# Attention loop of a recurrent-attention and mixture-of-experts kernel: the decay scans, the copies of T's blocks and one group of constants change their places and size

## The chip, the cores and the metric

One core of a Trainium2 chip. The metric is the device time of one execution in microseconds; lower is better. Engines: PE (TensorE), DVE (VectorE), ACT (ScalarE), POOL (GpSimd) and SP (SyncE, which issues most transfers).

## The reference

Three programs follow one another: a recurrent attention over 768 steps for 32 heads with a state of 40x40 each, a mixture of 8 experts with one expert for each token, and a dense network with squared ReLU.

```python
for t in range(S):
    y[:, :, t] = np.einsum('bhd,bhde->bhe', rt, state)
    Sa = np.einsum('bhde,bhe->bhd', state, at)
    state_decay = state * wt[:, :, None, :] - np.einsum('bhd,bhe->bhde', Sa, bt)
    state = state_decay + np.einsum('bhd,bhe->bhde', vt, kt)
...
x = np.ascontiguousarray(attn_out.transpose(0, 2, 1, 3)).reshape(B * S, H * D)
x = _moe_ref(x=x, **moe_kwargs)
return _moe2_ref(x=x, **moe2_kwargs)
```

## The kernel before

**Tiling.** The attention works in 24 chunks of 32 steps; all 32 heads of a chunk are treated together. Inside a chunk the recurrence becomes matrices of 32x32 per head. Of each chunk the kernel needs: the products of the decays from both ends of the chunk (`scan`, two scans on DVE of 104x512, L157 and L163, with L160 and L162 between them), the inputs scaled by them (`scale`, L175 to L177, three products on POOL; for m >= 2 L175 is DVE's), a gram matrix on PE with a mask (`gram` L191, `gram_mask` L206 on ACT and L207 on DVE), and the inverse T of a triangular matrix. T is worked out for four chunks at once, spread over four iterations (`inv_start`, `inv`: products L261 on DVE and POOL, sums L265 on DVE, and at the end a transpose on DVE, L300, into the tile TT). `block_T` (L309) copies the blocks of one chunk from TT into the block-diagonal tile TB with four copies on ACT; `solve` (L386, px) multiplies with it.

**Order.** The order of the instructions on every engine is the order in which the code is written (`manual_schedule`): no scheduler moves anything. Each engine takes its own instructions in that order and waits for others by semaphores. The loop in `run` goes over c from 0 to 22, m is c % 4, and LA is 7. Iteration c works on several chunks at once: the state, the scores and the output y of chunk c; T's use (`solve`) for chunk c+1; the natural-order copies (`nat_n`, `nat_a`) and `block_T` of chunk c+2; the gram of chunk c+7; the scan and the scaling of chunk c+8 (nothing from c=16 on, since there are 24 chunks).

**One iteration, in PE's order.** u1 (L401) and state_t (L453), nat_k (L337, pk), u (L417), solve (L386, px), state (L437, ps), vu_t (L467, pv), gram (L191), scores (L479, pq), the transposes of x for the gate (L805, gpt), a group of constants (L519, `warm`), the gate's logits (L819, pl), a second group of constants, y (L497), the transposes pa (L337), and a third group at the head of the next iteration; a fourth one stands ahead of u. `warm` multiplies a tile of constants and writes a tile of PSUM that nothing reads.

**ACT's order around the change.** The logits' copy (L820), two copies into X (L332, L333), the copies of pa (L349, L350, L358), T's blocks (L309, four copies into TB), then the next iteration's copies into ru (L406), rhsY (L457), vu (L422), rhsY (L375), lu (L389), vut (L470).

**DVE's order around the change.** The state's update (L441), the gram's mask (L207), the two scans, the mask of the scores (L483, which y needs as its operand rq), and then, by m: in m=0 the inverse's first products, with the scans behind the mask of the scores; in m=1 four sums of the inverse; in m=2 L175, the last sums and products and the transpose L300; in m=3 the gate's choice (L840 to L848), L175 and the ranks. At the end of an iteration stands x (L506). In m=3, and in some late iterations, PE counts the experts (L857, pc) between pa and the next u1, and ACT copies the counts (L859, pr).

**Queues.** SP loads the operands of later chunks (E, wB, R, V) in code order; a load waits until the readers of its buffer are done. POOL scatters the rows of x (L901).

Of the kernel before, what the change touches and what calls it, by code (L numbers as in the profile page):

```python
# [35 lines left out]
class Attention:  # L36
# [484 lines left out]
    def run(self, extra, weights):  # L521
        LA = 7
# [4 lines left out]
        def wload(i):  # L527
            r = (self.L, self.Tt)[i % 2].rearrange("p a b -> p (a b)")
            weights.load(i, r[:, 0:704], 1)
# [57 lines left out]
        idle = gate.mats.rearrange("p a b -> p (a b)")  # L587
        late, LM = None, 0

        def warm0(i):  # L590
            if c == 0:
                self.warm(W2[i], self.zt, 320, True)

        for c in range(NC - 1):
            m = c % 4
            warm0(0)
            bt = gate.batch(c)
            if c:
                self.warm(1, idle, 256, True)
            self.u1(c)  # L600
            if c:
                self.state_t(c)
            self.nat_k(c + 1)
            if c:
                self.warm(1, idle, 256, True)
            self.u(c)
            self.nat_kc(c + 1)
            self.solve(c + 1)
            if bt and 17 <= c:
                gate.choose(*bt)  # L610
            warm0(1)
            if c == 0:
                self.gram(5)
                self.gram_mask(5)
                self.scale(6, (V, G, V))
            if m:
                self.load_r(c + 1)
                self.load(c + LA + 2)
            if c in FILL:
                extra(*FILL[c])  # L620
            if c >= 21:
                gate.xT(c - 1)
            if c == 22:
                self.warm(1, idle, 256)
            self.state(c)
            if m == 0:
                self.load_r(c + 1)
                self.load(c + LA + 2)
            if c == 0:
                self.scan(7)  # L630
                self.scale(7, (V, G, G))
            self.vu_t(c)
            if c:
                self.gram(c + LA)
                self.gram_mask(c + LA)
                if m == 0:
                    self.inv_start(c // 4 + 1, lambda k, h: G)
                self.inv(PLAN[m][0])
            else:
                PLAN0 = PLAN[0][0] + PLAN[0][1]  # L640
                warm0(2)
                self.gram(6)
                self.gram_mask(6)
                warm0(3)
            if m:
                self.scan(c + LA + 1)
            self.scores(c)
            if c < 21:
                gate.xT(c - 1)
            if c:  # L650
                self.warm(1, idle, 256)
            gate.logits(c - 1)
            if c == 0:
                warm0(4)
                self.gram(7)
                self.gram_mask(7)
                warm0(5)
                self.inv_start(1, lambda k, h: G)
            if bt and c < 17:
                gate.choose(*bt)  # L660
            self.load_v(c + 2)
            if c:
                self.store_x(c - 1)
            if m == 0:
                self.scan(c + LA + 1)
            self.scale(c + LA + 1, (G, V, G) if m >= 2 else None)
            self.load_w(c + LA + 4)
            if bt:
                if c == 22:
                    self.warm(1, idle, 256)  # L670
                if c >= 17:
                    gate.count(*bt)
            if c:
                self.warm(1, idle, 512)
            self.y(c)
            self.nat_n(c + 2)
            self.nat_a(c + 2)
            self.nat_pc(c + 2)
            if bt and c < 17:
                gate.count(*bt)  # L680
            self.inv(PLAN[m][1] if c else PLAN0)
            self.block_T(c + 2)
            if late and m == LM:
                gate.rank_batch(*late)
            late = bt if bt and c < 17 else late if m != LM else None
            if c >= 21:
                self.gate_in(c, x22 if c == 22 else None)
            if bt:
                gate.rank(*bt)
                if 17 <= c < 22:  # L690
                    gate.rank_batch(*bt)
            if c < 21:
                self.gate_in(c)
            gate.scatter(1 if c < 20 else 2)
            for i in range(2):
                if 20 <= c < 22:
                    weights.prep(2 * c - 40 + i, i == 0)
                if 19 <= c < 21:
                    wload(2 * c - 38 + i)
            if c == 21:  # L700

                one, iota = (self.p2.tile([128, 512], F32, tag="wB", name=f"io{i}", bufs=3)[:, 0:NS1] for i in range(2))
                V.memset(one, 1.0)
                V.tensor_tensor_scan(iota, one, one, -1.0, ALU.mult, ALU.add)
                T1 = self.eb(6, [128, DM + 2 * NS1], F32)
                x22, oh22, oh23 = T1[:, 0:DM], T1[:, DM : DM + NS1], T1[:, DM + NS1 :]
        c = NC - 1
# [921 lines left out]
```

## Time and profile before

| what | value |
|---|---|
| median of 3 runs | 1175.13 us (1173.62 to 1182.4) |
| the profiled execution | 1179.27 us, of which the span from first to last instruction is 1177.6 us |
| busy over the span | PE 1022.5 us (87%), DVE 685.8 (58%), ACT 613.4 (52%), POOL 286.1 (24%) |
| mean granted TensorE clock | 0.925 of full speed |

All times in the rows below are from that one execution. An instruction group of a timeline row has its start, its length, engine, line, operation, output and inputs, count, and in brackets how long the engine was idle ahead of it and what ended that. PE's busy time counts pipelined matmuls whose ends are modelled. The granted clock is a share of 2.4 GHz; its only other level is 1.2 GHz (0.50), so a value between is a mix over the stretch.

### The profile page before, as it was taken

Reading aid. Unit: us, or ns where it says so; the run is one execution under the profiler, and the core shown is the slowest. Engines: PE = TensorE matmul, PEld = TensorE weight load, DVE = VectorE, ACT = ScalarE, POOL = GpSimd, SP = SyncE. Lnnn points to the kernel's source line nnn. Section 1 sums busy time; section 2 is a strip of 40 time slices with the busy share of each in tenths; the row PEclk is TensorE's granted clock in tenths of the full one; section 3 lists DMA queues with packets and bytes.
Section 4 is the critical chain, followed back from the end, with each engine's and each line's share of the span. In section 5 each row is a group of like instructions: output and inputs, shape, how many; then the busy total and the mean of one; then the engine's idle time right before and its main releaser. Section 6 shows DMA issues by size and latency. Waiting matters only on the chain.

```text
span 1177.6 us, 33048 instructions
## 1 busy us (share of the span) xinstructions
PE 1022.5 (87%) x13806; PEld 889.1 (76%) x13806; DVE 685.8 (58%) x1435; ACT 613.4 (52%) x1402; POOL 286.1 (24%) x338
## 2 busy tenths in 40 slices
PE   5376897787897888879988999989999999999996
PEld 3255676575676766667888999878899999999995
DVE  7964645675475364345688787886744444344432
ACT  7156457475565666852555555545644444444431
POOL 5423113123123120001265554541430101000000
PEclk7588869999789799997999999989999999999998
DMA  7737326344343122212676676652310101000000
GB/s 208 196 91 237 83 75 181 87 134 137 98 120 91 45 77 88 88 40 71 184 229 211 210 218 210 196 161 82 89 56 12 34 12 35 13 11 13 11 13 25
DMA packets 75087, 122.86 MB, mean 104 GB/s; under 512 B 8790, under 2 KB 56520, under 8 KB 72432
## 3 DMA queue, kind: packets, MB, share of 16 engines
q1 hardware_dynamic: 72624, 112.87, 33.1%
q0 software_dynamic: 2304, 7.78, 2.0%
q8 instruction: 110, 1.80, 0.6%
q14 instruction: 49, 0.40, 0.1%
HBM read 91.36 MB, written 29.35 MB: 103 GB/s over the span
## 4 chain that ended last, share of the span: by engine, by line
PE 56%; ACT 15%; DVE 12%; issue 5%; DMA 3%; POOL 1%; SPq 0%; ACTq 0%; DVEq 0%; POOLq 0%
PE phg L1292 15%; PE pog L1318 5%; PE pog L1317 5%; PE pog L1316 5%; PE phe L1292 4%; PE px L386 3%; ACT ru L406 3%; PE warm L519 2%; ACT TB L309 2%; ACT rhsY L457 2%; DVE e L163 2%; PE ps L437 2%; DVE rq L483 2%; ACT vut L470 1%; PE pa L337 1%
## 5 line engine op out<-in xcount | busy, mean ns | idle before, releaser
L1302 DVE SCALAR_TENSOR_TENSOR sqg<-phg,rg 128x512 f32<-128x512 f32 x96 | 66.3, 691 | 119.1 <-ACT rg L1301 115.6
L441 DVE TENSOR_TENSOR ru<-ps,Pc 40x640 f32<-40x640 f32 x46 | 37.8, 822 | 142.1 <-PE ps L437 141.7
L1301 ACT ACTIVATE rg<-phg 128x512 f32<-128x512 f32 x96 | 57.3, 596 | 110.7 <-PE phg L1292 110.5
L1304 DVE TENSOR_TENSOR hlg<-sqg,hhg 128x512 fp32r<-128x512 f32 x96 | 66.6, 694 | 65.9 <-ACT hhg L1303 61.1
L1303 ACT CAST hhg<-sqg 128x512 fp32r<-128x512 f32 x96 | 59.6, 620 | 78.6 <-DVE sqg L1302 75.4
L1292 PE MATMUL phg<-xhg,e 128*128 128x512 f32 x264 | 93.1, 393 | 0.0
L519 PE MATMUL warm<-mats 128*128 128x256 f32 x204 | 82.4, 496 | 1.4 <-ACT pr L859 1.4
L386 PE MATMUL px<-TB,X 128*112 128x128 f32 x384 | 59.9, 321 | 24.5 <-DVE N L207 15.3
L386 PEld LDWEIGHTS px<-TB,X 128*112 128x112 f32 x384 | 54.8, 216 | 27.4 <-DVE N L207 15.5
L1318 PE MATMUL pog<-e,hlg 128*128 128x320 f32 x240 | 74.2, 309 | 0.0
L1317 PE MATMUL pog<-e,hhg 128*128 128x320 f32 x240 | 74.1, 309 | 0.0
L1316 PE MATMUL pog<-e,hhg 128*128 128x320 f32 x240 | 74.0, 308 | 0.0
L176 POOL TENSOR_TENSOR e<-e,wB 104x512 f32<-104x512 f32 x21 | 35.7, 1700 | 121.3 <-PE warm L519 84.5
L1110 POOL TENSOR_TENSOR e<-rw,e 128x256 fp32r<-128x256 f32 x51 | 43.3, 853 | 70.0 <-ACT e L1109 56.0
L1292 PE MATMUL phe<-xhe,e 128*128 128x480 f32 (+4 forms) x176 | 59.2, 377 | 0.0
L1292 PEld LDWEIGHTS phg<-xhg,e 128*128 128x128 f32 x264 | 49.6, 188 | 8.9
L1318 PE MATMUL poe<-e,hle 128*120 128x320 f32 (+4 forms) x150 | 47.3, 316 | 5.9 <-DVE hle L1297 5.9
L1292 PE MATMUL phg<-xlg,e 128*128 128x512 f32 x132 | 51.8, 392 | 0.0
L1296 ACT ACTIVATE hhe<-phe 128x480 fp32r<-128x480 f32 (+4 forms) x64 | 33.8, 529 | 34.1 <-PE phe L1292 33.8
L1431 POOL DMA_INDIRECT x2g<-zs_s,idx x24 | 23.7, 988 | 113.6 <-ACT hhg L1303 105.7
L191 PE MATMUL G<-e 64*32 64x64 f32 (+1 forms) x1536 | 23.7, 245 | 29.3 <-issue 15.1
L417 PEld LDWEIGHTS pu<-ru,lu 128*32 128x32 f32 x1536 | 19.6, 125 | 38.7 <-ACT ru L406 32.3
(330 smaller groups left out, 2995.8 us busy)
## 6 DMA issues: line engine op xcount, KB each, us to landing
e<-in_E_dram SPq DMA_DIRECT2D x24, 832.0 KB
rw<-in_w_dram SPq DMA_DIRECT2D x30, 320.0 KB
rw<-in_w_dram SPq DMA_DIRECT2D x30, 256.0 KB
zs_s<-zt SPq DMA_DIRECT2D x4, 1600.0 KB
ru<-in_VR_dram SPq DMA_DIRECT2D x48, 128.0 KB
cr<-in_wi_dram SPq DMA_DIRECT2D x20, 256.0 KB
cr<-in_wo_dram SPq DMA_DIRECT2D x20, 256.0 KB
wB<-in_E_dram SPq DMA_DIRECT2D x23, 208.0 KB
```

The lines of the kernel that those rows point to most:

```text
L386: self.nc.tensor.matmul(px[0:112, par, 128 * o : 128 * o + 128], X[:, par, o, :], TB[:, 4 * par + o, :], start=True, stop=True)
L441: V.tensor_tensor(rUn[s, par, :, :, 0:40].rearrange("p (h q) z d -> p h (q z) d", h=2), ps[s, :, 0:320].rearrange("p h (a d) -> p h a d", ...
L519: self.nc.tensor.matmul(w[:, i % 2, 0:cols], r[:, 0:128], r[:, 0:cols], start=True, stop=True)
L1110: (V if own else self.nc.gpsimd).tensor_tensor(W["l1"], r1, b32(W["h1"]), ALU.subtract)
L1292: T.matmul(o, lt, rt, start=(i == 0), stop=(i == len(seq) - 1))
L1301: A.activation(r[:, :n], o, AF.Relu)
L1302: V.scalar_tensor_tensor(sq[:, :n], o, 0.0, r[:, :n], ALU.max, ALU.mult)
L1303: A.copy(hh[:, :n], sq[:, :n])
L1304: V.tensor_tensor(hl[:, :n], sq[:, :n], b32(hh)[:, :n], ALU.subtract)
L1316: T.matmul(o, hh[:, t], W["h2"], start=(f == 0), stop=False)
L1317: T.matmul(o, hh[:, t], W["l2"], start=False, stop=False)
L1318: T.matmul(o, hl[:, t], W["h2"], start=False, stop=(f == NF - 1))
```

## The change

Three edits in the loop of `run`. `scan(c + LA + 1)` stands, for every m, behind the scores, the logits, the gate's choice and the loads; before, only m=0 had it there, and m=1 to 3 had it ahead of the scores. `block_T(c + 2)` stands directly behind the logits for m=0, 1 and 3; for m=2 it stays behind the inverse, which ends there. The second group of constants, between the logits and y, has 256 columns instead of 512.

```diff
-            if m:
-                self.scan(c + LA + 1)
             self.scores(c)
             if c < 21:
                 gate.xT(c - 1)
             if c:
                 self.warm(1, idle, 256)
             gate.logits(c - 1)
+            if m != 2:
+                self.block_T(c + 2)
...
             if c:
                 self.store_x(c - 1)
-            if m == 0:
-                self.scan(c + LA + 1)
+            self.scan(c + LA + 1)
             self.scale(c + LA + 1, (G, V, G) if m >= 2 else None)
...
             if c:
-                self.warm(1, idle, 512)
+                self.warm(1, idle, 256)
             self.y(c)
...
             self.inv(PLAN[m][1] if c else PLAN0)
-            self.block_T(c + 2)
+            if m == 2:
+                self.block_T(c + 2)
```

DVE's rows in iteration c=5 (m=1), from the state's update to x, before (the scans are printed as SCALAR_TENSOR_TENSOR; rq is the masked scores, Xm an inner tile of the inverse):

```order
L441 TENSOR_TENSOR ru_119<-ps_2489,Pc_597 40x16x40 x2
L207 TENSOR_TENSOR N_2576<-G_2543,mL 128x384
L157 SCALAR_TENSOR_TENSOR wB_1591<-wB_1591,onesB 104x512
L160 TENSOR_TENSOR Pc_2586<-wB_1591,e_2167 104x16
L162 RECIPROCAL zR<-Pc_2586 104x16
L163 SCALAR_TENSOR_TENSOR e_2167<-e_2167,zR 104x512
L483 TENSOR_TENSOR rq_126<-pq_2590,mQ 64x512 x2
L265 TENSOR_REDUCE Xm<-pr_7_2579 128x32
```

and of the changed kernel:

```order
L441 TENSOR_TENSOR ru_119<-ps_2489,Pc_597 40x16x40 x2
L207 TENSOR_TENSOR N_2576<-G_2543,mL 128x384
L483 TENSOR_TENSOR rq_126<-pq_2585,mQ 64x512 x2
L157 SCALAR_TENSOR_TENSOR wB_1591<-wB_1591,onesB 104x512
L160 TENSOR_TENSOR Pc_2628<-wB_1591,e_2167 104x16
L162 RECIPROCAL zR<-Pc_2628 104x16
L163 SCALAR_TENSOR_TENSOR e_2167<-e_2167,zR 104x512
L265 TENSOR_REDUCE Xm<-pr_7_2579 128x32
```

The mask of the scores L483 stands directly behind the gram's mask L207, and the four rows of the scan follow it.

DVE's rows in iteration c=6 (m=2), up to the transpose into TT, before:

```order
L441 TENSOR_TENSOR ru_120<-ps_2818,Pc_783 40x16x40 x2
L207 TENSOR_TENSOR N_2905<-G_2872,mL 128x384
L157 SCALAR_TENSOR_TENSOR wB_1928<-wB_1928,onesB 104x512
L160 TENSOR_TENSOR Pc_2915<-wB_1928,e_2486 104x16
L162 RECIPROCAL zR<-Pc_2915 104x16
L163 SCALAR_TENSOR_TENSOR e_2486<-e_2486,zR 104x512
L483 TENSOR_TENSOR rq_125<-pq_2919,mQ 64x512 x2
L175 TENSOR_TENSOR e_2486<-e_2486,wB_1928 104x16x32
L265 TENSOR_REDUCE Tt<-pr_11_2908 128x8x4
L265 TENSOR_REDUCE Tt<-pr_12_2910 128x8x4
...
L300 STREAM_TRANSPOSE TT<-Tt 128x32x32
```

and of the changed kernel:

```order
L441 TENSOR_TENSOR ru_120<-ps_2818,Pc_783 40x16x40 x2
L207 TENSOR_TENSOR N_2905<-G_2872,mL 128x384
L483 TENSOR_TENSOR rq_125<-pq_2914,mQ 64x512 x2
L157 SCALAR_TENSOR_TENSOR wB_1932<-wB_1932,onesB 104x512
L160 TENSOR_TENSOR Pc_2953<-wB_1932,e_2486 104x16
L162 RECIPROCAL zR<-Pc_2953 104x16
L163 SCALAR_TENSOR_TENSOR e_2486<-e_2486,zR 104x512
L175 TENSOR_TENSOR e_2486<-e_2486,wB_1932 104x16x32
L265 TENSOR_REDUCE Tt<-pr_11_2908 128x8x4
L265 TENSOR_REDUCE Tt<-pr_12_2910 128x8x4
...
L300 STREAM_TRANSPOSE TT<-Tt 128x32x32
```

The same rows stand ahead of the transpose L300; L175 now follows the scan L163 directly, where the mask L483 stood between them.

ACT's rows from the last copy of pa in iteration c=4 to the copies into X in c=5, before:

```order
L358 COPY Pn_2327<-pa_2316 128x320
L309 COPY TB_117<-TT 32x8x32 x4
L406 COPY ru_120<-pu_2367 16x8x40 x4
...
L820 COPY lg<-pl_2618 128x8
L332 COPY X_114<-N_901 128x4x48
L333 COPY X_114<-N_901 128x4x48
```

and of the changed kernel:

```order
L358 COPY Pn_2331<-pa_2320 128x320
L406 COPY ru_120<-pu_2367 16x8x40 x4
...
L820 COPY lg<-pl_2613 128x8
L309 COPY TB_118<-TT 32x8x32 x4
L332 COPY X_114<-N_905 128x4x48
L333 COPY X_114<-N_905 128x4x48
```

Between the copy of pa L358 and L406 no block copies are left; those of the next chunk stand behind the logits' copy L820 and ahead of the copies into X.

## Rows read from the trace of the kernel before

**Rows 1.** The page: chain that ended last, whole span, by engine
```profile
PE 56%; ACT 15%; DVE 12%; issue 5%; DMA 3%; POOL 1%; SPq 0%; ACTq 0%; DVEq 0%; POOLq 0%
```

**Rows 2.** Waits, 150 to 520 us: engine, line, waited for: us, times, longest
```profile
ACT X L349 <- PE pa L337: 54.5, 18, 4.8
```

**Rows 3.** Stretches by iteration: us; PE, PEld, DVE, ACT, POOL busy; clock; DMA; GB/s
```profile
138.54:162.71 24.17, 21.78 (x445) 17.67 (x446) 10.78 (x29) 12.24 (x32) 3.71 (x3) 0.72 0.34 91
226.74:245.16 18.42, 15.84 (x443) 12.77 (x443) 11.31 (x31) 11.61 (x30) 3.54 (x3) 1.00 0.42 117
245.16:264.26 19.10, 15.75 (x435) 12.90 (x437) 17.41 (x37) 12.21 (x30) 7.44 (x7) 0.91 0.42 117
264.26:284.38 20.12, 14.89 (x435) 11.83 (x437) 8.88 (x17) 12.20 (x30) 7.78 (x7) 1.00 0.58 178
387.62:411.68 24.06, 21.78 (x445) 18.02 (x447) 11.29 (x30) 13.45 (x33) 4.51 (x4) 0.72 0.17 54
463.14:479.80 16.66, 13.84 (x371) 11.03 (x373) 4.81 (x14) 11.83 (x29) 0.98 (x1) 1.00 0.38 111
```

**Rows 4.** Timeline, c=9: start us, us, engine, line, instruction [idle before <-releaser]
```profile
267.15 0.76 PE L191 MATMUL G<-e 64*32 64x64 f32 x52 [1.49 <-issue]
270.60 1.93 DVE L163 TENSOR_TENSOR_SCAN e<-e,zR 104x512 f32<-104x512 f32 x1
270.94 1.12 PE L519 MATMUL warm<-mats 128*128 128x512 f32 x2
271.05 0.17 ACT L820 COPY lg<-pl 128x8 f32<-128x8 f32 x1 [1.02 <-PE pl L819]
271.50 0.35 ACT L333 COPY X<-N 128x192 f32<-128x192 f32 x1
272.45 1.38 DVE L483 TENSOR_TENSOR rq<-pq,mQ 64x512 f32<-64x512 f32 x2
273.55 1.27 POOL L177 TENSOR_TENSOR e<-e 104x512 f32<-104x512 f32 x1
274.60 0.93 PE L337 MATMUL pa<-ident,e 104*128 104x104 f32 x8
275.37 0.62 PE L519 MATMUL warm<-mats 128*128 128x256 f32 x2
275.92 0.84 PE L401 MATMUL pu<-ru,lu 128*16 128x40 f32 x64
276.26 1.65 ACT L309 COPY TB<-TT 32x256 f32<-32x256 f32 x4
277.81 1.70 ACT L406 COPY ru<-pu 16x320 f32<-16x320 f32 x4
```

**Rows 5.** Timeline, c=7, ACT
```profile
231.71 0.17 ACT L820 COPY lg<-pl 128x8 f32<-128x8 f32 x1 [1.02 <-PE pl L819]
235.97 0.29 ACT L349 COPY X<-pa 128x160 f32<-128x160 f32 x1 [3.47 <-PE pa L337]
238.59 1.70 ACT L406 COPY ru<-pu 16x320 f32<-16x320 f32 x4
```

**Rows 6.** Timeline, c=6, ACT and PE
```profile
217.13 1.64 ACT L309 COPY TB<-TT 32x256 f32<-32x256 f32 x4 [1.87 <-DVE TT L300]
220.44 0.80 PE L417 MATMUL pu<-ru,lu 128*32 128x40 f32 x64 [2.93 <-ACT ru L406]
221.85 3.49 PE L386 MATMUL px<-TB,X 128*112 128x128 f32 x16 [0.61 <-ACT rhsY L457]
```

**Rows 7.** Timeline, c=19, PE and ACT
```profile
471.34 0.77 PE L401 MATMUL pu<-ru,lu 128*16 128x40 f32 x64
473.23 1.70 ACT L406 COPY ru<-pu 16x320 f32<-16x320 f32 x4
```

**Rows 8.** Timeline, c=8, POOL and DVE
```profile
254.87 2.19 POOL L176 TENSOR_TENSOR e<-e,wB 104x512 f32<-104x512 f32 x1
255.91 1.20 DVE L261 TENSOR_TENSOR pr<-L,Tt 128x36 f32<-128x36 f32 x1
```

## The prediction

> **What bounds the kernel now.** I read the chain of work that ended last first [rows 1]. Over the whole span 56% of it is PE, 15% ACT and 12% DVE, but this is a mean over two programs: the change touches the attention loop alone. So the second view is who waited for whom in that loop [rows 2]: between 150 and 520 us ACT sat idle 54.5 us in 18 waits of up to 4.8 us for the transposes pa. ACT's copies of pa are the first link of what follows (ru, rhsY, vu, lu, vut: ACT without a gap until the next gram), so each of these waits lengthens an iteration.
>
> The third view is one row per iteration, from one state update (L441) to the next [rows 3]. Here c is the iteration and m is c % 4. The reader is to see two things. No engine is full in any row. And the length hangs on the clock: c=7 takes 18.42 us at a granted clock of 1.00 (2.4 GHz), c=3 24.17 and c=15 24.06 at 0.72, a mix of that and 1.2 GHz. There are three such long stretches (c=3, 11, 15).
>
> The fourth view is the timeline of one iteration of each kind. In c=9 (m=1) DVE runs the scans of a later chunk up to 272.45 and only then the mask of the scores, which ends at 273.83; y and pa (274.60) come behind it [rows 4]. ACT then copies pa, then T's blocks (276.26, 1.65 us), and only then reaches L406 (277.81), for which PE's L401 had been ready since 276.76.
>
> **The change part by part.** Call the iteration's gain the amount by which L406 starts earlier, since from there ACT runs without a gap.
>
> *T's blocks and 256 columns, where y waits for no scan.* In c=19 (no scan is left) L401 ends at 472.11 and L406 starts at 473.23 because the four block copies stand between [rows 7]. The group of 512 columns takes 1.12 us, one of 256 takes 0.62 [rows 4], so PE is 0.5 us earlier: L401 ends at 471.61, and L406 starts there, 1.6 us earlier. The copies themselves move into ACT's wait for pa. This holds for c=1, 4, 8, 12, 16, 17, 19, 20, 21: 9 x 1.6 = 14.4 us. In c=18 and 22 only the 0.5 us count: 1.0.
>
> *The scan behind the mask, m=1.* In c=9 the second scan alone runs 1.93 us from 270.60 [rows 4], and the first stands ahead of it; without both the mask can begin before 270, and it lasts 1.38 us (272.45 to 273.83). Then y waits for PE's own constants instead, 270.94 + 0.62 = 271.56, and pa follows 0.77 later (as 274.60 follows 273.83) at 272.33. L401 stands 1.32 us behind it and takes 0.84: 274.49. ACT meanwhile: logits copied at 271.22, blocks 1.65, two copies into X 0.63, so it is ready for pa at 273.50 and through with its copies (0.73, from pa's end at 275.53 to 276.26) before 274.49. L406 then starts at 274.5 instead of 277.81 [rows 4]: 3.3 us, for c=5, 9, 13: 9.9 us. What is late next is PE's row of constants, logits and constants; the scan is no longer in the chain.
>
> *m=3.* In c=7 the counting sits between pa and L401, and L406 starts 2.62 us behind the first copy of pa (235.97 to 238.59). With the blocks ahead, ACT is ready for pa at 231.88 + 1.64 + 0.63 = 234.15, so L406 comes 1.8 us earlier [rows 5]. Four such iterations (3, 7, 11, 15): 7.2 us.
>
> *m=2 with a scan (c=2, 6, 10, 14).* Here T's blocks stay where they are, behind DVE's transpose into TT, and DVE runs the same instructions up to it, only in another order. In c=6 ACT cannot copy a block before 217.13 [rows 6], now or then: no gain. It can lose: today the mask stands between scan and L175, and POOL's L177, released by the scan, runs beside the mask. Now L175 stands directly behind the scan. In c=8 a DVE product of 36 elements took 1.20 us beside a POOL product, and ended 0.05 us behind it [rows 8]. So one of the two may hold the other, for up to 1.2 us; I take 0.3, since DVE issues its L175 without a semaphore and only the product of 128x128 behind it can then meet the rest of L177. 4 x -0.3 = -1.2. The Trainium skill (SBUF — State Buffer, section "Who interferes with whom") says that a DVE instruction with two SBUF inputs contends with a GpSimd one that reads SBUF, and that issue order decides who is blocked. The row of c=8 agrees; by the worse order the sum would be 3.6 us less.
>
> *What waits longer.* In m=1 to 3 the scan ends about 1.4 us later after the gram's mask. Behind it in DVE's queue are L175, the inverse's totals, the ranks and xt; POOL's L177 waits for it, and the next gram for L177. In c=9 L177 ends at 274.82 [rows 4] and the next gram runs behind the next state update at 284.38 [rows 3], some 10 us later; 1.4 plus the 3.3 gained leave it covered. SP's order does not change; its load of wB waits for POOL and moves by the same 1.4 us. I cost this at nothing, with that cover.
>
> *PE's waits without a releaser.* In c=9 the gram stopped for 1.49 us with nothing in the profile to end it [rows 4]. If what ends such a wait is not moved by the change, the gain ahead of it is lost. I take off three gains of 1.6: -4.8; bounds 0 and -20, about two thirds of all the gains.
>
> *The clock.* PE idles 2.93 us before L417 in c=6, and px then takes 3.49 us [rows 6]. With y some 2.3 us earlier the idle stretch is 5.2 us in each m=2. c=6 pays for a shorter stretch already, so I take only 4 x -0.5 = -2, bounds 0 and -6. The Trainium skill (TensorE: Matmul & The Clock Gate, section "HAM oscillation — how this bites in real kernels") says that idle gaps between bursts of matmuls bring the lower clock back, and that every gap pays anew. The trace agrees in c=6; by it alone the sum would take the -6. In the other direction, c=3 and c=15 cost 5.75 and 5.64 us over c=7 [rows 3], 16.8 for the three. Their PE waited for the mask in the same way as c=9's, and in c=19, where no scan is ahead of the mask, the clock is 1.00. But c=7 was at 1.00 with the wait, and the constants that keep PE busy are halved, so I count one of the three as gone: +5.5, bounds 0 and +16.8.
>
> **Sum.** 14.4 + 1.0 + 9.9 + 7.2 - 1.2 = 31.3; less 4.8 and 2, plus 5.5: 30.0 us. The profiled execution took 1179.27 us (span 1177.6 and 1.7 around it), so 1149.3 against its own time. It lies 4.1 above the median of the runs, 1175.13; from there the forecast is 1145.1 us. The expert stage behind the loop only starts earlier.
>
> **The rivals.**
> 1. *All three long stretches at the lower clock go.* For: c=19 at 1.00 [rows 3], and PE no longer idle ahead of y. Against: half the constants. 31.3 - 2 + 16.8 = 46 us: 1129.
> 2. *DVE becomes the bound.* For: in c=8 DVE is busy 17.41 of 19.10 us [rows 3]. Then c=4, 8, 12 give nothing (-4.8), the m=1 that follow lose 1.7 each to a late state update (-5.1), and m=2 pays 1.2 instead of 0.3 (-3.6): 30.0 - 13.5 = 16.5, 1158.6. Against: DVE's next needed step, the state update, is not read until the next iteration's L401.
> 3. *The change doesn't do what it says:* the gains end at waits that do not move (loads, PE's unexplained stops). 30.0 - 20 = 10: 1165, within 1%.
> 4. *Slower: the clock falls with the constants.* The place is PE between the logits and px in m=0, 1 and 3, where 512 columns become 256. If PE is then granted 1.2 GHz through that stretch, an iteration costs 5.5 us more, as c=3 and c=15 do. Without the +5.5 the gain is 24.5, so from five such iterations beyond today's three the kernel is slower than before, from seven by over 1%; eight give 24.5 - 44 = -19.5, 1194.6. Against: PE's idle stretches get shorter in these iterations, by more than the 0.5 us of constants.
>
> **How the numbers follow.** Forecast 0.42, rival 1 0.22, rival 2 0.20, rival 3 0.11, rival 4 0.05. Faster by over 1% are the first three cases, 0.84; within 1% (about what a measurement of this kernel can tell from no change) rival 3, 0.11; slower 0.05. The range reaches from just beyond rival 1 to rival 3: 1127 to 1165; outside are half of rival 3, all of rival 4, and what lies beyond the three long stretches.
>
> **What would show it.** Right: DVE's mask directly behind the gram's mask with y waiting on PE in m=1 and 3; c=9 near 17 us instead of 20.12, c=19 near 15 instead of 16.66; m=2 as long as before; ACT's waits for pa down by more than half. Wrong: L406 still behind something other than L401; a granted clock under 0.8 in rows that had 1.00; the gram waiting for POOL; DVE without a gap ahead of L441 in m=1.

## The result, and the profile after

The changed kernel takes 1142.08 us (median of four runs, 1140.46 to 1160.43) beside 1178.77 us for the kernel before in the same session; the ratio is 0.9684, 95% interval 0.9617 to 0.975, with the run of 1160.43 us left out as disturbed. The profiled execution took 1140.46 us, span 1138.7, at a mean granted clock of 0.942 (before: 1179.27, 1177.6 and 0.925). The forecast was 1145.1 us, a gain of 30.0; by the medians the gain is 36.7. The total came near, but its term for the clock did not come out.

The page of the kernel after, first part (busy time) and chain that ended last:

```profile
PE 988.9 (87%) x13806; PEld 867.5 (76%) x13806; DVE 694.7 (61%) x1435; ACT 614.1 (54%) x1402; POOL 288.6 (25%) x338
PE 56%; ACT 13%; DVE 9%; issue 7%; DMA 4%; POOL 2%; SPq 1%; ACTq 0%; DVEq 0%; POOLq 0%
```

Against [rows 1], ACT and DVE give up 2% and 3% of the chain, and "issue", time in which an engine waits for nothing that the profile shows, takes 2% more. In the waits from 150 to 520 us the line of [rows 2] falls from 54.5 to 14.3 us. PE's longest wait in sum is still that of L417 for L406, but what were 14 waits of up to 2.9 us are now five of up to 5.5 us. Before, and then the two lines of the kernel after:

```profile
PE pu L417 <- ACT ru L406: 17.1, 14, 2.9
```
```profile
PE pu L417 <- ACT ru L406: 15.3, 5, 5.5
...
ACT X L349 <- PE pa L337: 14.3, 8, 3.2
```

Stretches of the kernel after, each from one state update (L441) to the next: c=3, 6, 7, 8, 9, 10, 14, 15, 19, columns as in [rows 3]:

```profile
135.26:151.70 16.44, 15.31 (x443) 12.69 (x441) 11.95 (x29) 11.53 (x30) 4.09 (x3) 1.00 0.39 110
188.71:212.77 24.06, 16.51 (x437) 13.93 (x439) 11.87 (x17) 13.30 (x31) 2.91 (x2) 0.86 0.30 89
212.77:229.27 16.50, 15.13 (x443) 12.64 (x444) 12.45 (x30) 11.62 (x30) 3.90 (x3) 1.00 0.36 103
229.27:250.07 20.80, 16.00 (x449) 13.47 (x449) 17.43 (x36) 12.84 (x31) 7.42 (x7) 0.92 0.48 131
250.07:267.46 17.39, 15.33 (x421) 12.58 (x417) 9.20 (x17) 11.69 (x28) 7.83 (x7) 0.90 0.56 184
267.46:291.91 24.45, 18.83 (x437) 15.72 (x439) 12.03 (x18) 13.41 (x32) 3.91 (x3) 0.79 0.38 104
...
343.30:366.23 22.93, 16.84 (x437) 14.31 (x439) 11.89 (x17) 13.41 (x32) 3.92 (x3) 0.85 0.17 52
366.23:382.73 16.50, 15.12 (x443) 12.63 (x443) 12.48 (x31) 11.63 (x30) 3.90 (x3) 1.00 0.23 69
435.51:450.68 15.17, 13.35 (x371) 11.04 (x373) 4.80 (x14) 11.94 (x29) 0.00 (x0) 1.00 0.39 111
```

Beside [rows 3], c=3 and c=15 fall from 24.17 and 24.06 us at a granted clock of 0.72 to 16.44 and 16.50 at 1.00, c=9 from 20.12 to 17.39, c=19 from 16.66 to 15.17; c=8 is slower, and so is m=2 but for c=2. From c=1 to c=21 the two traces differ by (c=0 takes the same time in both):

| kind | iterations | change, us |
|---|---|---|
| m=3 | 3, 7, 11, 15, 19 | -7.7, -1.9, -7.2, -7.6, -1.5: -25.9 |
| m=1 | 1, 5, 9, 13, 17, 21 | -0.9, -1.5, -2.7, -2.3, -0.3, -2.0: -9.7 |
| m=0 | 4, 8, 12, 16, 20 | -2.6, +1.7, -0.6, +0.4, -1.9: -3.0 |
| m=2 | 2, 6, 10, 14, 18 | -2.4, +1.1, +3.1, +2.6, +1.2: +5.6 |
| behind the loop | | -5.8 |

That is 38.8 us of the 38.9 between the two spans. In c=9, where y had waited for DVE, the instructions now follow one another as the prediction worked it out. Timeline of the kernel after, c=9, columns as in [rows 4]:

```profile
251.95 0.81 PE L191 MATMUL G<-e 64*32 64x64 f32 x52 [0.99 <-issue]
254.72 1.41 DVE L483 TENSOR_TENSOR rq<-pq,mQ 64x512 f32<-64x512 f32 x2 [0.94 <-PE pq L479]
256.98 0.70 PE L519 MATMUL warm<-mats 128*128 128x256 f32 x2
257.27 1.65 ACT L309 COPY TB<-TT 32x256 f32<-32x256 f32 x4
257.61 0.80 PE L497 MATMUL py<-rhsY,rq 128*32 128x40 f32 x64
257.93 1.95 DVE L163 TENSOR_TENSOR_SCAN e<-e,zR 104x512 f32<-104x512 f32 x1
258.34 0.93 PE L337 MATMUL pa<-ident,e 104*128 104x104 f32 x8
259.65 0.77 PE L401 MATMUL pu<-ru,lu 128*16 128x40 f32 x64
260.49 1.70 ACT L406 COPY ru<-pu 16x320 f32<-16x320 f32 x4 [0.24 <-PE pu L401]
```

The mask (L483) now ends at 256.13, while PE still has the logits and the second group of constants (L519) to do; y follows these, the blocks (L309) lie in ACT's wait for pa, and L406 waits for L401 and nothing else. It starts 10.42 us behind L441; before it was 13.55 (277.81 in [rows 4], less 264.26 in [rows 3]).

m=2 is where the change costs. Timeline of c=14, before:

```profile
382.80 0.80 PE L417 MATMUL pu<-ru,lu 128*32 128x40 f32 x64 [1.35 <-ACT ru L406]
384.21 2.00 PE L386 MATMUL px<-TB,X 128*112 128x128 f32 x16 [0.61 <-ACT rhsY L457]
```

and after:

```profile
351.84 1.64 POOL L177 TENSOR_TENSOR e<-e 104x512 f32<-104x512 f32 x1 [1.16 <-DVE e L163]
...
353.11 0.61 DVE L261 TENSOR_TENSOR pr<-Xm,Tt 128x128 f32<-128x128 f32 x1
...
356.08 1.64 ACT L309 COPY TB<-TT 32x256 f32<-32x256 f32 x4 [4.41 <-DVE TT L300]
359.38 1.29 PE L417 MATMUL pu<-ru,lu 128*32 128x40 f32 x64 [5.09 <-ACT ru L406]
360.79 3.76 PE L386 MATMUL px<-TB,X 128*112 128x128 f32 x16
```

y is earlier, T is not: ACT waits 4.41 us for DVE's transpose (0.58 in the same iteration before, 1.87 in c=6, [rows 6]), PE 5.09 us for L406, and behind that pause the lower clock level (1.2 of 2.4 GHz) is granted: from 359.38 to 366.23 the granted clock is 0.58, and px takes 3.76 us, where it takes 2.00 at the upper level.

### The profile page after: what moved, and what is told of

Its sections match the earlier page's. It is cut to its first block, busy times and chain, and to the rows that moved or that the text cites. A ratio compares the mean times of both kernels' runs of the same rounds, so it can differ in the third digit from the quotient of the medians.

```text
span 1138.7 us, 33048 instructions
## 1 busy us (share of the span) xinstructions
PE 988.9 (87%) x13806; PEld 867.5 (76%) x13806; DVE 694.7 (61%) x1435; ACT 614.1 (54%) x1402; POOL 288.6 (25%) x338
## 4 chain that ended last, share of the span: by engine, by line
PE 56%; ACT 13%; DVE 9%; issue 7%; DMA 4%; POOL 2%; SPq 1%; ACTq 0%; DVEq 0%; POOLq 0%
PE phg L1292 15%; PE pog L1318 5%; PE pog L1317 5%; PE pog L1316 5%; PE px L386 3%; PE phe L1292 3%; PE warm L519 3%; PE pq L479 2%; ACT ru L406 2%; DMA xs<-zs_s 2%; ACT rhsY L457 2%; PE ps L437 2%; ACT vu L422 1%; PE pl L819 1%; ACT TB L309 1%
## 5 line engine op out<-in xcount | busy, mean ns | idle before, releaser
L441 DVE TENSOR_TENSOR ru<-ps,Pc 40x640 f32<-40x640 f32 x46 | 37.8, 821 | 100.9 <-PE ps L437 100.5
L386 PE MATMUL px<-TB,X 128*112 128x128 f32 x384 | 55.7, 306 | 22.8 <-DVE N L207 15.3
L519 PE MATMUL warm<-mats 128*128 128x256 f32 x204 | 68.7, 427 | 2.9 <-ACT pr L859 1.9
L386 PEld LDWEIGHTS px<-TB,X 128*112 128x112 f32 x384 | 50.6, 202 | 25.5 <-DVE N L207 15.5
L309 ACT COPY TB<-TT 32x256 f32<-32x256 f32 x94 | 37.8, 402 | 27.5 <-DVE TT L300 26.2
L479 PE MATMUL pq<-rq,vut 128*64 128x64 f32 x768 | 34.3, 235 | 18.1 <-issue 10.7
```

The lines of the kernel that those rows point to most:

```text
L309: (copies[g] if copies else self.nc.scalar.copy)(self.TB[c % 2][t, :, t], self.TT[t, 8 * (c % 4) : 8 * (c % 4) + 8])
L386: self.nc.tensor.matmul(px[0:112, par, 128 * o : 128 * o + 128], X[:, par, o, :], TB[:, 4 * par + o, :], start=True, stop=True)
L479: T.matmul(pq[s, 64 * q : 64 * q + 64], vut[:, q, s], rt[:, :, q, pp], start=True, stop=True)
L519: self.nc.tensor.matmul(w[:, i % 2, 0:cols], r[:, 0:128], r[:, 0:cols], start=True, stop=True)
```

## The experiments

An interval is that of the ratio to the kernel before on the same chip. The kernel before moved between 1161 and 1184 us over the chips.

**The scans alone.** Both `self.scan` calls become one behind the mask; the rest is as before. The wait that is to go, in c=3 of the kernel before:

```profile
145.42 0.23 PE L497 MATMUL py<-rhsY,rq 128*32 128x40 f32 x2 [0.89 <-issue]
146.10 1.05 PE L497 MATMUL py<-rhsY,rq 128*32 128x40 f32 x62 [0.45 <-DVE rq L483]
```

PE stands 0.89 and 0.45 us around the first matmuls of y, and from 146.42 us on, for 13.65 us, it is granted the lower level: pa takes 1.65 us. In c=7 the same two waits (0.88 and 0.45 us) stand, and pa takes 0.93. (The first of the two waits is printed "issue", but ends when half of the mask is done.)

> Only the scans move behind the mask; the four block copies stay behind the inverse and the constants stay at 512 columns. Theory 1 (the scan set the clock of m=3: PE stood ahead of y behind DVE's scan, and this brought the three long stretches at the lower clock): c=3, 11 and 15 fall from about 24 us to 19 or less, with a granted clock of 0.95 or more in these rows, c=5, 9 and 13 give 1 to 2 us each, and the kernel comes out some 18 to 22 us below before. Theory 2 (the blocks set it: the late L406 left PE without work ahead of L417): c=3, 11 and 15 stay at 0.72 and 23 us or more, and the whole gain is 4 to 8 us, from m=1 alone.

Measured: 1158.79 us (before there 1170.29), ratio 0.9886 (0.9816 to 0.9956). c=3, 11 and 15, and mask and y of c=7:

```profile
140.16:156.89 16.73, 15.75 (x443) 12.73 (x444) 11.95 (x28) 11.52 (x30) 4.08 (x3) 1.00 0.38 111
297.55:314.34 16.79, 15.54 (x443) 12.63 (x443) 12.48 (x30) 11.59 (x30) 3.91 (x3) 1.00 0.39 109
374.79:391.61 16.82, 15.57 (x443) 12.66 (x443) 12.48 (x31) 11.62 (x30) 4.14 (x4) 1.00 0.24 67
```
```profile
221.37 1.41 DVE L483 TENSOR_TENSOR rq<-pq,mQ 64x512 f32<-64x512 f32 x2 [0.36 <-PE pq L479]
...
224.34 0.80 PE L497 MATMUL py<-rhsY,rq 128*32 128x40 f32 x64
```

The rows of m=3 are those of theory 1: all three long stretches go by the scan's move alone. Its other signs came in part. The total is 11.5 us below before by the medians (interval 5 to 22), where it named 18 to 22. Of m=1 only c=9 is shorter (17.84 us); c=5 and c=13 take 18.86 and 18.49, before 18.05 and 18.12. And m=2 already pays here: c=10 and c=14 take 23.04 and 22.93 us at 0.85, before 21.39 and 20.32.

**The blocks alone.** `if m != 2: self.block_T(c + 2)` behind the logits, the scans and 512 columns as before.

> Only the block copies move behind the logits (m not 2). Theory 1 (the scan set the clock): c=3, 11 and 15 keep a granted clock of about 0.72 and lose no more than 2 us; iterations of m=0 give 1 us each, and the whole comes out 8 to 14 us below before. Theory 2 (the blocks set it): the three rows rise to 0.95 or more, and the whole is 20 to 26 us below before. Both expect L406 to start directly behind L401 in c=19, about 1.1 us earlier.

Measured: 1167.33 us, 0.9951 (0.9913 to 0.999), by the ratio 5.7 us. The clock of m=3 stays low in three of four, though not the same three: c=3 18.35 us at 1.00, c=7 23.30 at 0.71, c=11 22.13 at 0.77, c=15 23.72 at 0.71 (the profile is of the longest of its ten runs). Theory 2 falls; the gain is below theory 1's 8 to 14, which the interval (1 to 10 us) just reaches. c=19 is 1.06 us shorter, as both expected.

**256 columns alone.**

```diff
-                self.warm(1, idle, 512)
+                self.warm(1, idle, 256)
             self.y(c)
```

> Only the constants ahead of y are halved. By the prediction's sum 0.5 us in each iteration where PE and not ACT is late, and nothing where L406 waits behind the block copies, as in c=19: 0 to 5 us below before. By rival 4 (halved constants cost the clock) more iterations show the lower clock through the stretch that c=3, 11 and 15 have, at 5.5 us each: 5 us or more above before.

Measured: 1175.77 us, 1.0055 (1.0021 to 1.009): slower by 0.2 to 0.9%. All four m=3 rows have the lower clock now, c=7 too, which had 1.00 before ([rows 3], 18.42 us):

```profile
224.53:248.01 23.48, 20.65 (x445) 17.41 (x447) 11.30 (x31) 12.85 (x32) 3.54 (x3) 0.71 0.35 95
```

Timeline of c=7:

```profile
229.15 1.93 DVE L163 TENSOR_TENSOR_SCAN e<-e,zR 104x512 f32<-104x512 f32 x1
231.01 1.38 DVE L483 TENSOR_TENSOR rq<-pq,mQ 64x512 f32<-64x512 f32 x2
231.76 0.31 PE L497 MATMUL py<-rhsY,rq 128*32 128x40 f32 x2 [1.43 <-issue]
232.44 1.29 PE L497 MATMUL py<-rhsY,rq 128*32 128x40 f32 x62 [0.36 <-DVE rq L483]
```

With the scan ahead of the mask, PE stands for 1.43 and 0.36 us around the first matmuls of y, where it had stood 0.88 and 0.45, and y and what follows it up to px run at the lower level (y 1.29 us where the run with the scans moved has 0.80). The rows are of the longest of the ten runs (1185.56 us), but the mean granted clock of all ten is 0.902 to 0.919, beside 0.913 to 0.941 of the kernel before there. Rival 4's mechanism exists while the scan stands ahead of the mask; with the scans moved, no m=3 row of the kernels with 256 columns shows it but two of the late-scan run below, which hold stops of another kind.

**The scans and the blocks, with 512 columns.**

> The whole change without its third part: 512 columns ahead of y again. By the sum it is slower than the changed kernel by 0.5 us in each of some 17 iterations in which PE is late behind y (all but m=2): 6 to 9 us, that is 22 to 29 us below before, with the granted clocks of the changed kernel. If the constants themselves hold the clock up, the low stretches at c=6, 10 and 14 get fewer and the kernel is no slower than the changed one, 32 us or more below before.

Measured: 1150.95 us, 0.9808 (0.9741 to 0.9875). The three rows are 16.79 to 16.89 us at 1.00, and m=2 stays low (c=10 0.85, c=14 0.85, c=6 0.79): the first theory's clocks. The total is less than the 22 to 29 us that were expected, within its interval. That interval shares only 0.9741 to 0.975 with the changed kernel's, but on another chip the changed kernel's median is at 0.9795 (next); the 0.5 us of each iteration is not shown in the total.

**The changed kernel again**, with the three runs that follow on one chip (before there: 1170.23).

> The changed kernel once more, beside the kernels below on one chip. Expected as in the result: 1140 to 1146 us, the rows of c=3, 7, 11 and 15 near 16.5 us at a granted clock of 1.00, those of c=6, 10 and 14 at 22.9 us or more with a clock under 0.90. If the low stretches of m=2 were chance, these rows come back near 21 us.

Measured: 1146.26 us, but its four runs reach from 1131.12 to 1158.61, and no interval can be given. c=3, 7, 11, 15 stand at 16.51 to 17.02 us and 1.00; c=6, 10 and 14 at 24.36, 26.03 and 22.13 with clocks of 0.80 to 0.86: a place, not chance.

**The scans of m=2 back ahead of the mask.**

```diff
+            if m == 2:
+                self.scan(c + LA + 1)
             self.scores(c)
...
-            self.scan(c + LA + 1)
+            if m != 2:
+                self.scan(c + LA + 1)
```

> The changed kernel with the scans of m=2 alone back ahead of the mask. Theory 1 (in m=2 the move costs: DVE stands idle for the scores before the mask, and its products run beside POOL's, so that the transpose of TT is not earlier while y is, and PE waits longer ahead of L417): c=6, 10, 14 and 18 go back to about 23, 21.4, 20.3 and 17.5 us, the wait ahead of L417 to about 3 us, 5 to 8 us below the changed kernel in all. Theory 2 (these rows lost the clock through the halved constants): they stay where they are, within 2 us in all.

Measured: 1142.36 us, 0.9747 (0.9672 to 0.9821), 3.9 below the changed kernel's median there, within its spread. The wait ahead of L417 falls to 1.22 us in c=14 and 0.93 in c=10, but the rows do not all follow: c=6 23.50, c=10 24.21, c=14 21.24, c=18 18.05. Neither theory holds alone. What PE waited less, it stood elsewhere: from 70 to 520 us its stops of 1 us or more without a releaser sum to 34.8 us here and 22.1 in the run above, those behind another engine to 5.0 and 24.7. Of the 34.8, 4.6 stand ahead of y in c=2, 6 and 14 and end with DVE's mask, whose wait is back there; 30.2 are left.

**The scans and scales of m=2 behind the inverse.**

```diff
-            self.scan(c + LA + 1)
-            self.scale(c + LA + 1, (G, V, G) if m >= 2 else None)
-            self.load_w(c + LA + 4)
+            if m != 2:
+                self.scan(c + LA + 1)
+                self.scale(c + LA + 1, (G, V, G) if m >= 2 else None)
+                self.load_w(c + LA + 4)
...
             if m == 2:
                 self.block_T(c + 2)
+                self.scan(c + LA + 1)
+                self.scale(c + LA + 1, (G, V, G))
+                self.load_w(c + LA + 4)
```

> The changed kernel with scan, scale and load of wB of m=2 behind the inverse and the block copies. Theory 1 (in m=2 the end of the inverse sets the iteration): the transpose into TT comes 4 us or more earlier in c=2, 6, 10 and 14, the wait ahead of L417 falls from 5 us to 1 or less, px is back at 2.0 us, and the kernel is 14 to 24 us below the changed one. Theory 2 (DVE is then late at the next step, the ranks, xt and the state update behind it): L441 behind c=2, 6, 10 and 14 starts without idle time on DVE, or the gram waits for POOL's L177, and no more than 4 us come out.

Measured: 1138.68 us, 0.9678 (0.96 to 0.9757). In c=6 and c=14 what theory 1 expects is there (18.11 and 16.47 us, 1.20 and 0.75 us ahead of L417, px 2.00); in c=2 px takes 3.33 us behind a wait of 1.11. The total is 7.6 us below the changed kernel's there, within its spread, where theory 1 named 14 to 24. The profiled run is the longest of the four, 1153.94 us, so it shows where a long execution loses time, not what the median loses; in it the stops without a releaser sum to 37.9 us, the longest from c=1 on 4.50 us ahead of L479 in c=8. DVE, theory 2's bound, idles 3.47 us ahead of L441 behind c=14.

**Constants in PE's pause.** In m=3, four groups of 512 columns ahead of L417 instead of one of 256: `self.warm(4 if m == 3 else 1, idle, 512 if m == 3 else 256, True)`. In the rows this stands at the end of c=2, 6, 10, 14 and 18.

> The changed kernel with four groups of 512 columns of constants, instead of one of 256, ahead of L417 in each m=3, where PE has no work for 5 us. Theory 1 (this idle time is what brings the lower clock to px and the state update in c=6, 10 and 14): px falls from 3.5 to 3.8 us to about 2.0 and these rows lose 1.5 to 3 us each, 5 to 9 us in all, although the constants themselves last 4.5 us. Theory 2 (the clock falls for another reason): px stays over 3 us; L417 comes up to 2 us later in c=10, where only 2.25 us were idle, and in c=18, and the kernel is 0 to 6 us above the changed one.

Measured: 1153.37 us, 0.9855 (0.9793 to 0.9917), above the changed kernel's median. In c=14 px falls to 2.00 and the row to 20.64 us at 1.00, as theory 1 says; in c=6 px takes 3.67 us in spite of the constants, c=10 is 25.27. In c=10 no pause is left and px is 2.00 too, but the row holds a stop of 3.43 us without a releaser. Inconclusive on the clock: a pause of 2.0 us stays in c=14, 2.55 in c=6. It brings no gain: the median is 7.1 us above the changed kernel's there, though within its spread, and part of that is stops (5.05 us in c=12) that the constants need not have caused.

**The load of E cut down.** This kernel leaves out three quarters of each load of E from chunk 9 on, so it computes other numbers. What PE waits for in a stop "<-issue" the waits do not tell. In c=8 of the kernel after, SP issues the load of E (832 KB, L137) at 225.40, and then:

```profile
230.35 0.85 PE L191 MATMUL G<-e 64*32 64x64 f32 x64 [0.49 <-issue]
234.99 1.30 PE L479 MATMUL pq<-rq,vut 128*64 128x64 f32 x27 [3.79 <-issue]
```
```profile
227.00:229.00 2.00, 2.00 (x70) 1.87 (x71) 0.00 (x0) 1.95 (x4) 0.55 (x1) 1.00 0.93 247
...
231.00:232.00 1.00, 0.20 (x21) 0.17 (x5) 0.35 (x1) 0.60 (x2) 0.00 (x0) 1.00 0.94 208
234.00:235.00 1.00, 0.01 (x2) 0.01 (x2) 0.83 (x5) 0.00 (x0) 0.00 (x0) 1.00 0.32 108
```

The last column but one is the DMA share: it is 0.70 to 0.94 in every us from 226 to 233, 0.94 in the one in which the stop begins (231.20), and 0.32 in the last one of the stop. The queue that the page calls "q8 instruction" moves 110 packets of 16 KB in the whole run. Its packets' times beside PE's restart, from the trace's DMA records:

| kernel after | packet, us | PE restarts | behind the packet's end | start of the packet before |
|---|---|---|---|---|
| c=4, L191, stop 1.67 | 152.21 to 153.53 | 154.93 | 1.40 | 6.8 us earlier |
| c=8, L479, stop 3.79 | 232.53 to 233.65 | 234.99 | 1.34 | 9.4 |
| c=10, L479, stop 1.81 | 269.57 to 270.58 | 272.19 | 1.61 | 5.9 |
| c=13, L191, stop 1.88 | 326.50 to 327.79 | 329.15 | 1.36 | 6.6 |

Of the 14 such stops in the kernel with the late scan, 13 end 1.26 to 1.70 us behind a packet of this queue. The other is one of about 4 us in c=0 that most of the kernels have and that ends 2.7 us or more behind a packet. So PE seems to wait for its own instructions, and these to stand behind the loads.

```diff
-        e = self.eb(c % 8, [104, 2048], F32)
-        self.nc.sync.dma_start(e, self.E[c][:, 0:2048])
+        if c < 8:
+            self.st["B", c] = self.eb(c % 8, [104, 2048], F32)
+        e, z = self.st["B", c % 8], 1536 if c >= 9 else 0
+        self.nc.sync.dma_start(e[:, z:2048], self.E[c][:, z:2048])
```

> The changed kernel with three quarters of each load of E left out from chunk 9 on (832 KB becomes 208 KB; the first 1536 columns keep what an earlier chunk left there, so the numbers computed from them are other ones). Theory 1 (PE's stops without a releaser are waits for its own instructions, whose 16 KB packets stand behind the load of E in the DMA engines): the stops of 1 us or more in the loop fall from about 20 us in all to under 8, the one of 3.8 us ahead of L479 in c=8 goes, c=8 takes 18 us or less, packets of PE's instruction queue lie at most 9 us apart, and the kernel is 10 to 20 us below the changed one. Theory 2 (the stops belong to PE's own program and have nothing to do with the loads): 15 us or more of stops stay, and the time stays within 4 us.

Measured: 1122.81 us (1122.4 to 1124.34), 0.9578 (0.9521 to 0.9635). The stops without a releaser sum to 7.8 us (4.3 of them the one in c=0), those of c=4 to c=14 to 1.3, where the changed kernel has 10.5; the runs lie within 2 us where the changed kernel's spread over 20 and more. By the ratios it is 12 us below the changed kernel, which ran on other chips; the two intervals share 0.9617 to 0.9635. Theory 1 holds but for two signs: c=8 takes 19.10 us, not 18, and packets of the queue still lie up to 11.8 us apart, not 9. c=8, c=12 and c=10:

```profile
223.47:242.57 19.10, 16.43 (x533) 13.71 (x535) 17.41 (x36) 14.77 (x34) 7.45 (x7) 1.00 0.42 131
295.06:314.11 19.05, 16.16 (x521) 13.33 (x523) 17.35 (x36) 14.47 (x34) 7.43 (x7) 1.00 0.32 91
255.61:278.55 22.94, 15.88 (x437) 13.45 (x439) 11.90 (x17) 13.32 (x31) 3.93 (x3) 0.85 0.26 77
```

c=10 has a clock of 0.85 without any stop of this kind, behind a wait of 5.48 us ahead of L417: m=2's price is another thing.

**The load of E in two halves.** The load takes columns 0 to 1023 where it stood; the rest follows behind the store of x:

```diff
...
-                self.load(c + LA + 2)
+                self.load(c + LA + 2, (0, 1024))
...
                 self.store_x(c - 1)
+            self.load(c + LA + 2, (1024, 2048))
```

> The changed kernel with each load of E from chunk 9 on in two halves of 416 KB: the first 1024 columns where the load stands now, the others behind the store of x, some 5 us later. Theory 1 (as above): the stop ahead of L479 in c=8 falls to 2 us or less and the sum of the stops by a third; 3 to 8 us below the changed kernel. Theory 2: no change within 3 us. If the second half meets PE's instructions in its turn, the stops move to L497 and L337 behind it, and nothing comes out.

Measured: 1133.38 us (before there 1174.44), 0.9635 (0.9554 to 0.9716). The stop in c=8 is 2.04 us, the sum 13.2 instead of 19.7 (from c=4 to c=14 3.1 instead of 10.5), both as theory 1 says, and this in the longest of its four runs; the total's interval overlaps that of the changed kernel.

**Both: late scan in m=2, and halves.**

> Late scan and scale of m=2, as in the run before, and the loads of E in halves. Theory 1: the 38 us of stops without a releaser that stood in the profile of the kernel with the late scan, where its gain went, fall to 25 or less, and the whole is 30 to 45 us below before, 4 us or more below the kernel with the late scan alone. Theory 2: 1138 us again, with 30 us or more of such stops.

Measured: 1116.15 us, 0.9462 (0.9378 to 0.9547), 58 us below before, more than the 30 to 45 that theory 1 named; the interval lies clear of the late scan's alone. The stops sum to 10.6 us. c=6, 10 and 14 take 16.77, 16.70 and 16.61 us at 1.00; c=2 still has 18.13 at 0.91. Timeline of c=14, line numbers one higher:

```profile
329.53 2.12 DVE L301 STREAM_TRANSPOSE TT<-Tt 128x1024 f32<-128x1024 f32 x1
331.54 1.18 DVE L158 TENSOR_TENSOR_SCAN wB<-wB,onesB 104x512 f32<-104x512 f32 x1
...
334.99 0.80 PE L418 MATMUL pu<-ru,lu 128*32 128x40 f32 x64 [0.53 <-ACT ru L407]
336.40 2.00 PE L387 MATMUL px<-TB,X 128*112 128x128 f32 x16 [0.61 <-ACT rhsY L458]
```

The transpose stands ahead of the scan, PE pauses 0.53 us, and px has its 2.00 us.

**And the ranks of m=0 one iteration later.** `late, LM = None, 1` instead of 0.

> Late scan of m=2 and loads of E in halves, as in the run before, and the second half of the ranks (eleven small DVE operations, 3.0 us, which stand ahead of xt and the state update in m=0) one iteration later, in m=1, where DVE stands idle for 5 us ahead of the state update. Theory 1 (in m=0 DVE is the bound: L441 starts without idle time behind these operations): c=4, 8 and 12 fall from 18.6 to 19.1 us to 16.5 to 17, m=1 keeps its time within 0.5 us, and the kernel is 5 to 8 us below the one of the run before, near 1110 us. Theory 2 (PE or ACT is as late as DVE there): the rows of m=0 stay above 18 us and nothing comes out.

Measured: 1118.48 us, 0.9533 (0.9491 to 0.9576): no gain. c=4 and c=8 fall as theory 1 says, to 16.56 and 16.57 us, c=12 only to 18.30, and the next iteration takes most of it back. c=8 and c=9 without and with the edit:

```profile
221.86:240.95 19.09, 15.86 (x531) 13.46 (x533) 17.39 (x37) 14.67 (x34) 7.43 (x7) 1.00 0.50 150
240.95:255.51 14.56, 13.03 (x343) 10.30 (x338) 9.07 (x16) 9.92 (x24) 7.79 (x7) 1.00 0.65 206
```
```profile
220.41:236.98 16.57, 14.12 (x435) 11.82 (x437) 14.69 (x25) 12.43 (x30) 6.54 (x6) 1.00 0.44 111
236.98:252.90 15.92, 14.53 (x433) 11.90 (x433) 14.20 (x27) 12.33 (x29) 8.73 (x9) 1.00 0.75 246
```

33.65 and 32.49 us together; c=4 with c=5 take 34.88 and 35.26, c=12 with c=13 34.24 and 34.34. In this trace c=14 is longer, too: 20.01 us at 0.83, with a stop of 1.77 us without a releaser. A late state update lengthened only the row, since PE went on past it (matmul instructions, the x behind PE's time: 531 and 343 without, 435 and 433 with).

## Why the prediction came out, and where it did not

- **T's blocks and 256 columns.** In c=19, L406 starts 8.60 us behind L441, before 10.09: 1.49 us, computed 1.6. The nine iterations were to give 14.4, less 4.8 for PE's waits without a releaser; they gave 7.6. The gain of c=8 was lost to the stop of 3.79 us ahead of L479: the term of 4.8 was right in kind, and the runs with the load of E cut down and halved showed that most of these stops hang on that load.
- **m=1.** L406 of c=9 moved by 3.13 us, computed 3.3; the chain L519, L497, L337, L401, L406 stands link by link. The three rows gave 6.5 of 9.9: c=5 and c=13 took 18.04 and 18.12 us before, c=9, from which the term was read, 20.12.
- **m=3.** In c=7 L406 starts 9.94 us behind L441 instead of 11.85: 1.91, computed 1.8.
- **m=2.** L261's product took 0.61 us beside POOL's L177 of 1.64, where before it had 0.38 and L177 1.27; T came 0.57 us later in c=14, taken at 0.3: 0.23 of it is this product, and 0.24 is DVE's wait for the scores ahead of the mask, which the prediction left out. The pause ahead of L417 is 5.1 to 5.5 us in c=2, 6 and 14 (forecast 5.2; before 2.95, 2.93 and 1.35); in c=10 it stayed, 2.25 behind 2.40. px went from 2.96, 3.49, 2.99 and 2.00 us to 3.11, 3.75, 3.46 and 3.76: 2.6 in all, forecast 2, bound 6. The Trainium skill's "HAM oscillation — how this bites in real kernels" (TensorE: Matmul & The Clock Gate), by which the lower clock is paid for anew in each iteration with such a gap, has its sign in these four, but not at the price of 6. Nor does every gap pay here: px took 2.00 us behind 1.35 in c=14 before, behind 0.75 and 1.20 in the late-scan run, and behind 2.03 in the run with constants. The whole of m=2 lost 5.6 where 2.7 was taken.
- **The clock: the step that failed** is "I count one of the three as gone: +5.5". All three long stretches at the lower clock went, rival 1's +16.8: m=3 without c=19 gave 24.4 us, and 7.2 + 16.8 is 24.0. The scans alone do it, the blocks alone do not. In every kernel with all scans, or all but those of m=2, behind the mask these rows have 1.00, but for c=3 and c=11 of the late-scan run (0.85 and 0.91), which hold stops of 3.0 and 1.4 us without a releaser. The prediction saw the wait ahead of y and counted its price in one of three, for two reasons. That c=7 had 1.00 in spite of the wait is true, but with 256 columns and a wait longer by half a microsecond it fell as well; why it alone kept the upper level before is not shown (with the blocks alone moved it was c=3 that kept it). That the constants are halved cost the clock only where the scan stayed ahead of the mask. Rival 1 had the condition right and not the time, 1129: its sum leaves out the 4.8 us of PE's waits without a releaser, with which it gives 1134, and the other terms were smaller than computed.
- **How the total still came out.** 11.3 us more from the stretches stand against 3.4 less in m=1, 2.9 in m=2, 2.0 in the nine and 0.5 in c=22 (not seen): 33 us instead of 30 in the loop. That these errors nearly cancel is luck. The 5.8 us behind the loop, where fewer stretches have the lower clock, were not forecast, and can't be put down to the change: over the 14 kept traces that part takes 651.0 to 656.8 us, 654.2 with the scans alone moved and 656.6 with the load in halves. And the median before came out 3.6 us above the one that the forecast starts from, which brings 1145.1 and 1142.08 nearer to each other than 30.0 and 36.7 are.
- **Rival 2, DVE the bound**, has its sign: L441 behind c=4, 8 and 12 starts without idle time on DVE (so it did behind c=8 before), and c=8 and c=12 take 19.1 us even without stops. But moving 3.0 us off DVE there gained nothing: the prediction's reason against it (the update is not read until L401) holds.
- **Rival 4** was right for the third part alone: 256 columns with the scan still ahead of the mask cost 0.2 to 0.9%. The parts do not add: -11.5, -3.0 and +5.5 us on one chip (medians), while the scans and the blocks together gave -19.3.

Still open: why c=7 kept the upper level before, whether 512 or 256 columns are better behind the moved scan, and what in the late-scan run brought back the lower clock in rows with stops, the stop itself or what runs behind it.

## What to carry to other kernels

Price a wait of TensorE by what is granted behind it, not by its own length: rows with a wait of 1.1 to 1.4 us at y were 7 us shorter without it in three cases of four, and 1.6 us in the fourth. And moving the same DVE work later made a new pause where DVE's result sets the end, so move it behind that result too. When waits vanish and the time does not, sum the stops without a releaser, take out those that end with another engine's result all the same, and set the rest beside the packets of the instruction queue; a large load issued in one piece may be what they stand behind. Judge an iteration by pairs of rows where an engine can run past the line that cuts them.

## What the runs showed of the hardware

PE stands still for up to 5.6 us with no wait in the profile, and restarts 1.2 to 1.7 us behind a 16 KB packet of an instruction queue; ahead of the stop in c=8 the DMA engines were busy to 0.7 to 0.94 while a load of 832 KB was under way. With a quarter of that load 1.3 us of such stops were left from c=4 to c=14, with the load in halves 3.1, of 10.5. And a pause that is taken away seems partly paid back in such stops: 24.7 and 22.1 us (behind engines, without a releaser) became 5.0 and 30.2 when m=2's pause went, as if the instructions had caught up during it. That last reading was not tested by itself.
